# Hashed attention with a mixture of adapters: turning the outputs on TensorE, scaling the signs as a product, and one written-out list of steps

## The chip, the cores and the metric

One Trainium2 chip, of which the kernel uses one core. The metric is the device time of one execution in microseconds (us); for the kernel before it is the median of three runs, and one further execution was profiled.

## The reference

Four batches of eight heads, 768 positions, 64 columns a head. Each row of q and k falls into one of 64 buckets by the signs of six projections; a row attends only to keys of its own bucket. The eight heads of a position are then put side by side as a row x of 512, which goes through the best two of eight adapters of rank 16.

```python
q_bits = (einsum('bhsd,dk->bhsk', q, proj) > 0)      # likewise k_bits; six bits make a bucket
mask = q_bucket[:, :, :, None] == k_bucket[:, :, None, :]
scores = where(mask, scale * q @ k.T, -1e9)
attn_out = softmax(scores) @ v
x = attn_out.transpose(0, 2, 1, 3).reshape(B * S, H * D)
logits = x @ w_gate                                  # 8 experts, the best two, softmax over the two
out = x + sum over the two of  w * ((x @ A[e]) @ B[e])
```

## The kernel before

**Pairs and tiles.** Two heads of a batch make a pair; there are 16 pairs, four to a batch. The scores of all pairs are cut into 144 tiles of 128 x 1024 (`score`, L337), nine to a pair. A tile is made by TensorE in one of three PSUM buffers `s` and turned by ScalarE (ACT) into exponentials in bfloat16 (L343), in the order of the tiles. Tiles 126 to 143 belong to pairs 14 and 15, whose rows are taken in three groups (three, two and one blocks of 128) in turn, so that the last batch can be routed group by group.

**What a tile contracts.** A tile's operands lie in `aug`, with 71 rows: 64 of q or k, and rows 64 to 70 with signs. The signs of the six projections are scaled (`sign`, L201 and L205) so that a pair of rows that differ in a bit gets a large negative score and its exponential vanishes. There are three `aug` buffers beside pair 0's own.

**Preparing a pair.** q and k are loaded in their natural layout (`loadqk`, buffers `nat`), turned in 32 x 32 blocks by VectorE (DVE; `turn32`, L179), cast to bfloat16 by GpSimd (POOL; `rcast`, L232, buffers `rb`) and brought to `aug` by four DMAs (`move`, L241). The projections are float32 products on TensorE (`hash`, L191, in the PSUM pool `n`). The scaled signs reach `aug` through DRAM (`sout`, L211, then `signs`, L218); pairs 0 and 1 bring them straight from SBUF by four DMAs (`sigd`, L221). Pair 0's head 0 has a way of its own (`f0`, `c0`, `g0`, `s0`, `k0`).

**After the exponentials.** Each head's products with v (`pvk`, L358; `pvg`, L378 for the groups) are summed in the PSUM pool `v`, opened by `uni` (L349, L367), a product with 2^-56 that covers rows without a partner. v is cast and summed by POOL (`vcast`, L165 to L170). `norm` (L423, L425) divides into x, in float32, and frees the bank. `to_bf` (L441, POOL) casts a finished pair's 128 columns to `xb`, and `turn` (L432) brings them to `xT` by a crossbar DMA transposition; the groups of the last two pairs are turned by TensorE instead (`turng`, L406) and copied by DVE (L407).

**Routing.** For three blocks of a batch at a time: `lgz` (L451) gives the logits and x A; `route1`, `route_exp` and `route2` find the best two and scale (L462 to L496); `zt` turns the scaled part on TensorE (L509) and copies it (L512); `delta` multiplies by B (L521) and adds x (L525); `store` writes 512 KB or 256 KB.

**What sets the order.** There is no scheduler: each engine takes its instructions in the order in which Python emits them, and waits for what an instruction needs. `plan` attaches steps to tiles (step s of pair p stands behind tile 9p + s), a pair's preparation runs in the two pairs before it (`prep`), and `HEAD`, `LAST` and `END` are lists for the start and the end. Nearly all DMAs go out from SyncE's queue (SP), where a waiting DMA holds all behind it. The pools `n` and `v` have one bank-sized buffer each, `s` three.

Of the kernel before, what the change touches and what calls it, by code (L numbers as in the profile page):

```python
# [22 lines left out]
class Emitter:  # L23


    def __init__(self, ctx, tc, q, k, v, proj, w_gate, A, Bm, out):
# [169 lines left out]
    def sign(self, p, r=slice(0, 128)):  # L196
# [8 lines left out]
        nc.vector.tensor_scalar(out=s2[r], in0=sg[r], scalar1=self.ssc[r], scalar2=None, op0=ALU.mult)  # L205
# [140 lines left out]
    def uni(self, p, h):  # L346
        T, D = self.T, self.D
        pv = self.pv[p, h] = self.ps_v.tile([self.P, T, D + 1], F32, tag="v", name=f"pv{p}_{h}")
        self.nc.tensor.matmul(out=pv, lhsT=self.eps,  # L349
                              rhs=self.vb[p % 3][:, h, T:T + 1, :].to_broadcast([self.P, T, D + 1]),  # L350
                              start=True, stop=False, skip_group_check=True)
# [47 lines left out]
    def turng(self, p, g, where=None):  # L399
        nc, P = self.nc, self.P  # L400
        b, hp = p // self.PPB, p % self.PPB
        i0, n = self.G[g]
        pool, tag = self.bank(where or "n")
        ps = pool.tile([P, n, P], BF16, tag=tag, name=f"xt{p}_{g}")
        for e in range(n):
            nc.tensor.transpose(out=ps[:, e, :], in_=self.xb[p, g][:, e, :], identity=self.ident_bf)  # L406
        nc.vector.tensor_copy(out=self.xT[b][:, hp, i0:i0 + n], in_=ps)  # L407
# [20 lines left out]
    def turn(self, p):  # L428
        if p < 0:
            return  # L430
        b, hp = p // self.PPB, p % self.PPB
        self.nc.sync.dma_start_transpose(out=self.xT[b][:, hp, :, :],  # L432
                                         in_=self.xb[p].rearrange("p t f -> p (t f)"))
# [45 lines left out]
    def route2(self, b, I):  # L479
        if b < 0:  # L480
            return
        nc, P, E, r, n = self.nc, self.P, self.E, self.r, len(I)
# [4 lines left out]
        zm = self.zm[b, I] = self.smallp.tile([P, n, self.ER], BF16, tag=f"zm{n}", name=f"zm{b}_{I[0]}")  # L487
        for i in range(n):
            nc.vector.tensor_tensor(  # L489
                out=zm[:, i, :].rearrange("p (e r) -> p e r", e=E),  # L490
                in0=lz[:, i, E:].rearrange("p (e r) -> p e r", e=E),
                in1=gw[:, i, :].unsqueeze(2).to_broadcast([P, E, r]), op=ALU.mult)
# [4 lines left out]

    def zt(self, b, Is, pool=None):
        if b < 0:
            return  # L500
# [1 line left out]
        n = sum(len(I) for I in Is)
        pool, tag = self.bank(pool or "n")
        ps = pool.tile([P, n, P], BF16, tag=tag, name=f"ztp{b}_{Is[0][0]}")
        zT = self.smallp.tile([P, n, P], BF16, tag=f"zT{n}", name=f"zT{b}_{Is[0][0]}")
        o = 0
        for I in Is:
            for j, i in enumerate(I):
                nc.tensor.transpose(out=ps[:, o, :], in_=self.zm[b, I][:, j, :], identity=self.ident_bf)  # L509
                self.zT[b, i] = (zT[:, o, :], self.rt[b, I][:, j:j + 1])  # L510
                o += 1
        nc.vector.tensor_copy(out=zT, in_=ps)  # L512

    def delta(self, b, i, pool=None):
        if b < 0:
            return
        nc, P = self.nc, self.P
        zT, rt = self.zT[b, i]
        pool, tag = self.bank(pool or "n")
        ps = pool.tile([P, self.Dm], F32, tag=tag, name=f"dl{b}_{i}")  # L520
        nc.tensor.matmul(out=ps, lhsT=zT, rhs=self.Bcat, start=True, stop=True)  # L521
# [3 lines left out]
        nc.vector.scalar_tensor_tensor(out=self.acc[b, u][:, e, :], in0=ps, scalar=rt,  # L525
                                       in1=self.x[b][:, i, :], op0=ALU.mult, op1=ALU.add)
# [201 lines left out]
```

## Time and profile before

| | |
|---|---|
| median of three runs | 192.81 us (190.43 to 193.36) |
| the profiled execution's own time | 191.84 us |
| its span, first to last instruction | 190.0 us |
| mean granted TensorE clock | 0.920 |
| TensorE products busy | 160.2 us, 2059 instructions |
| ScalarE busy | 142.6 us, 164 instructions |
| GpSimd busy | 112.5 us |
| VectorE busy | 110.4 us, 310 instructions |
| first and last exponential start | 8.86 us and 173.9 us |
| moved by DMA | 35.98 MB |

Times in the rows are counted from the span's start. A row of the timeline gives start, length, engine, line of the kernel, operation, output and inputs with their shape and the count; in brackets stands how long the engine was idle before it and who ended that. `PEld` is the loading of weights, `SPq` the issuing of DMAs. A busy TensorE is not TensorE at its peak: products are pipelined, and a row's length has the tail of the last one in it.

### The profile page before, as it was taken

What the parts mean: (1) busy time and instruction counts of PE and PEld (TensorE: products, weight loads), DVE (VectorE), ACT (ScalarE), POOL (GpSimd) and SP (SyncE); (2) the same over time, 40 slices, a digit from 0 to 9 for tenths busy, and PEclk for the clock granted to TensorE, in tenths of its full rate; (3) what the DMA queues carried; (4) which work ended last, traced back from release to release, by engine and by line L of the source; (5) the groups of instructions that cost most, each with busy time, mean ns of one, the idle gap of its engine ahead of it and who ended that gap; (6) DMA issues with size and microseconds to landing.
All of it is one profiled execution on the core that took longest, in us unless ns stands there. A gap on an engine that the chain in (4) does not pass through costs nothing.

```text
span 190.0 us, 5180 instructions
## 1 busy us (share of the span) xinstructions
PE 160.2 (84%) x2059; PEld 106.2 (56%) x2059; DVE 110.4 (58%) x310; ACT 142.6 (75%) x164; POOL 112.5 (59%) x152
## 2 busy tenths in 40 slices
PE   7784989599999979898898997998898998799350
PEld 2432555436576728585666583775666677587210
DVE  4666075411666543757877657087768363868671
ACT  3544759665999996999989989379898997796000
POOL 2879935787789158779590765868754955311000
PEclk9999699855999999999999999589999999999955
DMA  5962369597996969696879999897489782441205
GB/s 144 286 237 49 85 206 292 127 245 119 193 187 142 274 117 298 118 282 153 263 179 265 246 300 170 227 215 250 114 284 292 239 174 85 153 190 39 112 0 221
DMA packets 52836, 35.98 MB, mean 189 GB/s; under 512 B 37060, under 2 KB 49740, under 8 KB 52812
## 3 DMA queue, kind: packets, MB, share of 16 engines
q1 hardware_dynamic: 47756, 35.18, 68.8%
q0 software_dynamic: 4832, 0.27, 4.3%
q8 instruction: 16, 0.26, 0.6%
q10 hardware_dynamic: 224, 0.20, 0.4%
q14 instruction: 8, 0.07, 0.1%
HBM read 20.02 MB, written 6.98 MB: 142 GB/s over the span
## 4 chain that ended last, share of the span: by engine, by line
PE 44%; DVE 19%; DMA 16%; SPq 6%; POOL 5%; issue 4%; ACT 2%; DVEq 0%; POOLq 0%
PE s L337 18%; PE pv L358 9%; DMA aug<-rb 8%; PE hs L191 6%; DMA dr<-s 5%; DVE acc L525 3%; SPq L241 3%; DMA vn<-in_v_dram 3%; DVE R L179 3%; POOL rb L232 2%; PE lz L451 2%; DVE zm L489 2%; PE pv L349 2%; DVE s L205 2%; ACT P L343 2%
## 5 line engine op out<-in xcount | busy, mean ns | idle before, releaser
L343 ACT ACTIVATE P<-s 128x1024 bf16<-128x1024 f32 (+1 forms) x147 | 138.3, 1030 | 28.3 <-PE s L337 27.4
L337 PE MATMUL s<-aug 71*128 71x256 bf16 (+3 forms) x396 | 85.0, 328 | 4.3 <-DMA aug<-rb 3.8
L358 PEld LDWEIGHTS <-P 128*128 128x128 bf16 x1008 | 44.9, 102 | 16.1 <-issue 6.3
L232 POOL CAST rb<-R 128x768 bf16<-128x768 f32 (+1 forms) x32 | 47.5, 1491 | 7.1 <-DVE R L179 6.9
L337 PEld LDWEIGHTS <-aug 71*128 71x128 bf16 x396 | 39.3, 130 | 20.9 <-issue 14.1
L358 PE MATMUL pv<-vb,P 128*128 128x65 bf16 x1008 | 47.3, 199 | 0.0
L165 POOL CAST vb<-vn 128x768 bf16<-128x768 f32 x16 | 13.3, 832 | 36.5 <-DMA vn<-in_v_dram 27.9
L179 DVE STREAM_TRANSPOSE R<-nat 128x384 f32<-128x384 f32 x62 | 31.2, 548 | 2.4 <-DMA nat<-in_k_dram 1.9
L423 DVE RECIPROCAL ri<-pv 128x6 f32<-128x6 f32 x28 | 5.2, 187 | 33.4 <-PE pv L358 33.4
L191 PE MATMUL hs<-R,hst 128*32 128x192 f32 x248 | 20.1, 356 | 4.3 <-DVE zT L512 2.6
L525 DVE SCALAR_TENSOR_TENSOR acc<-dl,rt,x 128x512 f32<-128x512 f32 x24 | 17.5, 744 | 7.1 <-PE dl L521 6.9
L201 DVE TENSOR_SCALAR sg<-hs 128x192 bf16<-128x192 f32 (+1 forms) x16 | 5.7, 358 | 19.0 <-PE hs L191 19.0
L425 DVE TENSOR_TENSOR x<-pv,ri 128x384 f32<-128x384 f32 x28 | 15.6, 557 | 1.0
L167 POOL TENSOR_TENSOR vs<-vn 128x384 f32<-128x384 f32 x16 | 16.0, 1003 | 0.0
L191 PEld LDWEIGHTS hs<-R,hst 128*32 128x32 f32 x248 | 5.9, 111 | 16.0 <-issue 7.4
L349 PE MATMUL pv<-vb,eps 128*128 128x390 bf16 x28 | 9.9, 355 | 4.9 <-DVE x L425 2.7
L441 POOL CAST xb<-x 128x768 bf16<-128x768 f32 x14 | 11.5, 825 | 2.0 <-DVE x L425 1.9
L451 PE MATMUL lz<-wa,xT 128*128 128x136 bf16 x96 | 10.1, 235 | 3.0 <-DVE xT L407 2.5
L205 DVE TENSOR_SCALAR s<-sg,ssc 128x192 bf16<-128x192 bf16 (+1 forms) x16 | 12.3, 768 | 0.6
L521 PE MATMUL dl<-Bcat,zT 128*128 128x512 bf16 x24 | 9.4, 410 | 1.0 <-DVE zT L512 0.5
L397 POOL CAST xg<-x 128x384 bf16<-128x384 f32 (+2 forms) x5 | 2.1, 422 | 12.5 <-DVE x L391 12.5
L451 PEld LDWEIGHTS <-xT 128*128 128x128 bf16 x96 | 6.7, 103 | 3.6 <-issue 2.3
(61 smaller groups left out, 106.3 us busy)
## 6 DMA issues: line engine op xcount, KB each, us to landing
vn<-in_v_dram SPq DMA_DIRECT2D x16, 384.0 KB
nat<-in_q_dram SPq DMA_DIRECT2D x15, 384.0 KB
nat<-in_k_dram SPq DMA_DIRECT2D x15, 384.0 KB
aug<-rb SPq DMA_DIRECT2D x60, 96.0 KB
out_dram<-acc SPq DMA_DIRECT2D x11, 512.0 KB
dr<-s SPq DMA_DIRECT2D x14, 48.0 KB
aug<-dr SPq DMA_DIRECT2D x14, 42.0 KB
out_dram<-acc SPq DMA_DIRECT2D x2, 256.0 KB
```

Of the source, the lines that this page charges most:

```text
L167: nc.gpsimd.tensor_add(out=s3, in0=vn[:, :, 0:3, :], in1=vn[:, :, 3:6, :])
L179: self.nc.vector.transpose(out=self.R[p][:, i, :, h].rearrange("p f t c -> p t f c"), in_=self.nat[p][:, i, h, :].rearrange("p (t f c) -> ...
L191: nc.tensor.matmul(out=self.hs[p][32 * j:32 * j + 32], lhsT=self.hst[:, hf].rearrange("p b i -> p (b i)"), rhs=self.R[p][:, i, hf, h].rear ...
L205: nc.vector.tensor_scalar(out=s2[r], in0=sg[r], scalar1=self.ssc[r], scalar2=None, op0=ALU.mult)
L232: (eng or self.nc.gpsimd).tensor_copy(out=self.rb[p][:, :, :, i].rearrange("p f h (c t) -> p f h c t", t=self.T), in_=self.R[p][:, i, :, h ...
L337: nc.tensor.matmul(out=ps[:, c:c + w * P], lhsT=lhsT, rhs=rhs, start=True, stop=True)
L343: nc.scalar.activation(out=self.P_[p][:, o:o + b - a], in_=ps[:, a:b], func=ACT.Exp, scale=scale)
L349: self.nc.tensor.matmul(out=pv, lhsT=self.eps, rhs=self.vb[p % 3][:, h, T:T + 1, :].to_broadcast([self.P, T, D + 1]), start=True, stop=Fal ...
L358: self.nc.tensor.matmul(out=self.pv[p, h][:, i, :], lhsT=self.P_[p][:, o:o + P], rhs=self.vb[p % 3][:, h, kt, :], start=False, stop=(kt == ...
L425: nc.vector.tensor_tensor(out=self.x[b][:, :, c:c + D], in0=pv[:, :, 0:D], in1=ri.unsqueeze(2).to_broadcast([P, T, D]), op=ALU.mult)
L451: nc.tensor.matmul(out=self.lz[b, I][:, I.index(i), :], lhsT=self.xT[b][:, t, i, :], rhs=self.wa[:, t, :], start=(t == 0 and i == I[0]), s ...
L525: nc.vector.scalar_tensor_tensor(out=self.acc[b, u][:, e, :], in0=ps, scalar=rt, in1=self.x[b][:, i, :], op0=ALU.mult, op1=ALU.add)
```

## The change

Three edits.

1. `turn` is gone. `xtp` turns a pair's six 128 x 128 blocks on TensorE into a PSUM buffer of pool `n` or `s`, and `xtc` copies them to `xT` with DVE. This holds for pairs 0 to 13; the groups of pairs 14 and 15 were turned so before, and their step is now split in the same way (`xtpg`, `xtcg`).
2. In `sign` the scaling is a product of two tensors, the signs and a broadcast column, in place of a tensor by a scalar from memory.
3. `plan`, `prep`, `HEAD`, `LAST` and `END` are replaced by one list, `STEPS`, in which every step of the kernel but the first loads and constants stands in its place. Some steps are cut finer: `route2` into `gate`, `zmul` (one block each) and `gsum`; `zt` into `ztt` and `ztc`; `delta` into `dmm` and `dadd`; `pvk` by one key block. `hash`, `uni`, `unig`, `xtp`, `ztt` and `dmm` take their PSUM pool by name.

```diff
-        nc.vector.tensor_scalar(out=s2[r], in0=sg[r], scalar1=self.ssc[r], scalar2=None, op0=ALU.mult)
+        n = r.stop - r.start
+        nc.vector.tensor_tensor(out=s2[r], in0=sg[r], in1=self.ssc[r].to_broadcast([n, 192]), op=ALU.mult)
...
-    def turn(self, p):
-        self.nc.sync.dma_start_transpose(out=self.xT[b][:, hp, :, :],
-                                         in_=self.xb[p].rearrange("p t f -> p (t f)"))
+    def xtp(self, p, where):
+        pool, tag = self.bank(where)
+        ps = self.xt[p] = pool.tile([P, T, P], BF16, tag=tag, name=f"xt{p}")
+        for t in range(T):
+            nc.tensor.transpose(out=ps[:, t, :], in_=self.xb[p][:, t, :], identity=self.ident_bf)
+
+    def xtc(self, p):
+        b, hp = p // self.PPB, p % self.PPB
+        self.nc.vector.tensor_copy(out=self.xT[b][:, hp], in_=self.xt[p])
...
     def run(self):
         self.start()
-        plan = self.plan()
-        for n in range(9 * self.N):
-            self.score(n)
-            for f, *a in plan.get(n, ()):
-                getattr(self, f)(*a)
-        self.end()
+        for f, *a in STEPS:
+            getattr(self, f)(*a)
...
+STEPS = [
...
+    ("score",81), ("norm",8,0), ("dmm",0,5,"n"),
+    ("score",82),
+    ("score",83), ("turn32",11,1,0), ("dadd",0,5), ("turn32",11,1,1), ("uni",8,1), ("pvk",8,1,(0,)),
...
+]
```

The start on SP's queue. `s21` and `s22` are the scaled signs of pairs 1 and 2, `dr1` and `dr2` their place in DRAM, `rb` the cast rows, `nat` and `vn` the loads of q, k and v. Before:

```order
L221 DMA augf_117<-s20_244 7x4x192 x2
L241 DMA augf_117<-rb0_239 64x2x192 x4
L221 DMA aug1_119<-s21_282 7x4x192 x4
L241 DMA aug1_119<-rb1_268 64x4x192 x4
L146 DMA nat3_321<-in_q_dram 128x2x384
L146 DMA nat3_321<-in_k_dram 128x2x384
L211 DMA dr2_403<-s22_401 128x192
L146 DMA nat4_422<-in_q_dram 128x2x384
L146 DMA nat4_422<-in_k_dram 128x2x384
L241 DMA aug2_120<-rb2_319 64x4x192 x2
L157 DMA vn2_446<-in_v_dram 128x2x384
L218 DMA aug2_120<-dr2_403 7x4x768
```

and in the changed kernel:

```order
L214 DMA dr1_339<-s21_284 128x192
L147 DMA nat3_341<-in_q_dram 128x2x384
L147 DMA nat3_341<-in_k_dram 128x2x384
L221 DMA aug1_119<-dr1_339 7x4x768
L244 DMA aug1_119<-rb1_354 64x4x192 x4
L147 DMA nat4_382<-in_q_dram 128x2x384
L214 DMA dr2_394<-s22_352 128x192
L147 DMA nat4_382<-in_k_dram 128x2x384
L158 DMA vn2_426<-in_v_dram 128x2x384
L244 DMA aug2_120<-rb2_378 64x4x192 x4
L221 DMA aug2_120<-dr2_394 7x4x768
```

Pair 1's signs go through DRAM with the loads of pair 3 between the two steps, and pair 2's four moves stand together, ahead of its signs. (Ahead of these rows the loads of v 0 and v 1 have changed places with those of q and k, and a move of pair 0 stands ahead of `nat2`'s k.)

SP's queue around pairs 10 and 11 in the changed kernel; `acc0_1` is a piece of batch 0's output:

```order
L147 DMA nat12_1975<-in_k_dram 128x2x384
L147 DMA nat13_2042<-in_q_dram 128x2x384
L244 DMA aug2_120<-rb11_1970 64x4x192
L221 DMA aug1_119<-dr10_2000 7x4x768
L244 DMA aug1_119<-rb10_1795 64x4x192
L147 DMA nat14_2150<-in_q_dram 128x2x384
L147 DMA nat13_2042<-in_k_dram 128x2x384
L553 DMA out_0_dram<-acc0_1_1771 128x2x512
```

Before, each pair's loads, its signs, a transposition and its four moves followed one another in a fixed pattern, and no move of a later pair stood ahead of an earlier one's; here a move of pair 11 stands ahead of the signs and the last move of pair 10.

The end on DVE, where the last batch is routed. `dl3_2` is the product of its block 2, `xt15_1` the turned second group of pair 15, `top3_3` begins the routing of blocks 3 and 4. Before:

```order
L525 SCALAR_TENSOR_TENSOR acc3_1_3301<-dl3_2_3299,rt3_0_3217,x3_2615 128x512
L407 COPY xT3_2616<-xt15_1_3303 128x256
L462 MAX top3_3_3316<-lz3_3_3307 128x8 x2
L464 TENSOR_TENSOR d3_3_3319<-lz3_3_3307,top3_3_3316 128x16
L467 TENSOR_TENSOR m3_3_3321<-lz3_3_3307,top3_3_3316 128x16
```

and in the changed kernel:

```order
L415 COPY xT3_2688<-xt15_1_3380 128x256
L394 RECIPROCAL ri14_g2_3396<-pv14_g2_3373 128x2
L396 TENSOR_TENSOR x3_2687<-pv14_g2_3373,ri14_g2_3396 128x128
L475 MAX top3_3_3410<-lz3_3_3401 128x8 x2
L477 TENSOR_TENSOR d3_3_3413<-lz3_3_3401,top3_3_3410 128x16
L480 TENSOR_TENSOR m3_3_3415<-lz3_3_3401,top3_3_3410 128x16
L415 COPY xT3_2688<-xt14_2_3429 128x128
L394 RECIPROCAL ri15_g2_3438<-pv15_g2_3419 128x2
L396 TENSOR_TENSOR x3_2687<-pv15_g2_3419,ri15_g2_3438 128x128
L542 SCALAR_TENSOR_TENSOR acc3_1_3445<-dl3_2_3394,rt3_0_3346,x3_2687 128x512
```

The add of block 2 stood ahead of the copy and of the routing; now it follows both.

More of the change, by code (lines that the diff above doesn't have):

```diff
@@ L397, in normg, with xtpg, xtcg @@
             (nc.gpsimd if eng == "pool" else nc.vector).tensor_copy(out=xb, in_=xv)
-    def turng(self, p, g, where=None):
+    def xtpg(self, p, g, where):
         nc, P = self.nc, self.P
+        n = self.G[g][1]
+        pool, tag = self.bank(where)
+        ps = self.xt[p, g] = pool.tile([P, n, P], BF16, tag=tag, name=f"xt{p}_{g}")
+        for e in range(n):
+            nc.tensor.transpose(out=ps[:, e, :], in_=self.xb[p, g][:, e, :], identity=self.ident_bf)
+    def xtcg(self, p, g):
         b, hp = p // self.PPB, p % self.PPB
         i0, n = self.G[g]
[L403 to L407, printed above, removed]
+        self.nc.vector.tensor_copy(out=self.xT[b][:, hp, i0:i0 + n], in_=self.xt[p, g])
     def newx(self, b):
@@ L486, in route2 @@
         nc.vector.tensor_mul(out=gw, in0=m, in1=e)
[L487 to L492, printed above, removed]
+        self.rg[b, I] = gw
+        self.zm[b, I] = self.smallp.tile([P, n, self.ER], BF16, tag=f"zm{n}", name=f"zm{b}_{I[0]}")
@@ L495, in route2 @@
-        rt = self.rt[b, I] = self.smallp.tile([P, n], F32, tag=f"rt{n}", name=f"rt{b}_{I[0]}")
+        nc.vector.tensor_reduce(out=ss, in_=self.rg[b, I], axis=AX.X, op=ALU.add)
+        rt = self.smallp.tile([P, n], F32, tag=f"rt{n}", name=f"rt{b}_{I[0]}")
         nc.vector.reciprocal(out=rt, in_=ss)
-    def zt(self, b, Is, pool=None):
-        if b < 0:
-            return
-        nc, P = self.nc, self.P
[L502 to L521, printed above, removed]
+        for j, i in enumerate(I):
+            self.rt[b, i] = rt[:, j:j + 1]
+    def ztt(self, b, I, where):
+        nc, P, n = self.nc, self.P, len(I)
+        pool, tag = self.bank(where)
+        ps = self.ztp[b, I] = pool.tile([P, n, P], BF16, tag=tag, name=f"ztp{b}_{I[0]}")
+        for j in range(n):
+            nc.tensor.transpose(out=ps[:, j, :], in_=self.zm[b, I][:, j, :], identity=self.ident_bf)
@@ new lines, in ztc, with dmm @@
+    def ztc(self, b, I):
+        n = len(I)
+        zT = self.smallp.tile([self.P, n, self.P], BF16, tag=f"zT{n}", name=f"zT{b}_{I[0]}")
+        self.nc.vector.tensor_copy(out=zT, in_=self.ztp[b, I])
+        for j, i in enumerate(I):
+            self.zT[b, i] = zT[:, j, :]
+    def dmm(self, b, i, where, n=1):
+        nc, P = self.nc, self.P
+        pool, tag = self.bank(where)
+        ps = pool.tile([P, n, self.Dm], F32, tag=tag, name=f"dl{b}_{i}")
+        for j in range(n):
+            nc.tensor.matmul(out=ps[:, j], lhsT=self.zT[b, i + j], rhs=self.Bcat, start=True, stop=True)
+            self.dl[b, i + j] = ps[:, j]
```

390 lines of the change are left out of this document (265 added, 125 removed), and 9 rows, old and new, of tables (HEAD, STEPS).

## The prediction

> **What bounds the kernel now.** I read the page first: busy shares, the 40 slices with the granted clock.
>
> ```profile
> span 190.0 us, 5180 instructions
> PE 160.2 (84%) x2059; PEld 106.2 (56%) x2059; DVE 110.4 (58%) x310; ACT 142.6 (75%) x164; POOL 112.5 (59%) x152
> PEclk9999699855999999999999999589999999999955
> ```
>
> No engine fills the span. ACT has 142.6 us of work, nearly all of it the exponentials of 144 score tiles; PE comes next; and the clock falls to half in slices 5, 9, 10 and 26 (5 means half speed). So I read next ACT's timeline, where each row after a gap says what ACT waited for.
>
> ```profile
> 25.16 1.02 ACT L343 ACTIVATE P<-s 128x1024 bf16<-128x1024 f32 x1 [2.39 <-PE s L337]
> 35.95 2.08 ACT L343 ACTIVATE P<-s 128x1024 bf16<-128x1024 f32 x2 [1.70 <-PE s L337]
> 38.53 1.02 ACT L343 ACTIVATE P<-s 128x1024 bf16<-128x1024 f32 x1 [0.49 <-PE s L337]
> 40.04 1.02 ACT L343 ACTIVATE P<-s 128x1024 bf16<-128x1024 f32 x1 [0.49 <-PE s L337]
> 46.97 24.30 ACT L343 ACTIVATE P<-s 128x1024 bf16<-128x1024 f32 x26 [0.49 <-PE s L337]
> 72.84 3.10 ACT L343 ACTIVATE P<-s 128x1024 bf16<-128x1024 f32 x3 [1.58 <-PE s L337]
> 121.45 1.02 ACT L343 ACTIVATE P<-s 128x1024 bf16<-128x1024 f32 x1 [2.34 <-PE s L337]
> 126.42 3.76 ACT L343 ACTIVATE P<-s 128x1024 bf16<-128x1024 f32 x4
> 136.95 4.72 ACT L343 ACTIVATE P<-s 128x1024 bf16<-128x1024 f32 x5 [0.52 <-PE s L337]
> 146.14 4.72 ACT L343 ACTIVATE P<-s 128x1024 bf16<-128x1024 f32 x5 [0.52 <-PE s L337]
> 154.16 2.84 ACT L343 ACTIVATE P<-s 128x1024 bf16<-128x1024 f32 x3
> ```
>
> Counting the tiles row by row, 25.16 starts tile 9 (the first of pair 1), 35.95 tile 18 (pair 2), 46.97 tile 25, 72.84 tile 51, 126.42 tile 99, 154.16 tile 126 (the last two pairs). The 26 tiles from 46.97 took 24.30 us: **0.935 us a tile is ACT's own pace**. Against it the span divides into a head (to 25.16), tiles 9 to 51 (47.68 us for 42 tiles, 39.3 at ACT's pace), tiles 51 to 126 (81.32 us for 75, or 1.084 each), and the end (35.84 us from 154.16 to 190.0).
>
> Two stalls with a clock drop behind them stand out. From tile 18 seven tiles took 46.97 - 34.25 = 12.7 us instead of 6.5 (34.25 is 35.95 less the idle 1.70): **6.2 us lost**. From 119.11 (121.45 less 2.34) three tiles took 7.3 us instead of 2.8: **4.5 us lost**. What they waited for:
>
> ```profile
> 30.33 2.47 SPq L241 DMA_DIRECT2D aug<-rb  x2
> 35.24 0.61 PE L337 MATMUL s<-aug 71*128 71x512 bf16 x3 [2.25 <-DMA aug<-rb]
> 109.81 6.13 DMA vn<-in_v_dram
> 118.97 0.48 PE L349 MATMUL pv<-vb,eps 128*128 128x390 bf16 x1 [0.91 <-POOL vb L170]
> 116.00:117.00 1.00, 1.00 (x14) 0.30 (x18) 0.56 (x1) 0.94 (x2) 0.94 (x2) 1.00 1.97 47
> ```
>
> Pair 2's last two pieces of aug were issued at 30.33 and PE stood 2.25 us. In the second stall v's load took 6.13 us to land, POOL cast it late and PE's first product with it waited. The window's last columns are DMA share and GB/s: the queues were full at 47 GB/s while a crossbar transposition was among them.
>
> **What PE needs.** Starts of neighbouring rows give the cost without the pipeline's tail.
>
> ```profile
> 111.16 0.52 PE L451 MATMUL lz<-wa,xT 128*128 128x136 bf16 x6
> 111.52 1.03 PE L337 MATMUL s<-aug 71*128 71x256 bf16 x6
> 127.84 0.33 PE L509 MATMUL ztp<-ident_bf,zm 128*128 128x128 bf16 x3
> 128.01 0.60 PE L337 MATMUL s<-aug 71*128 71x512 bf16 x3
> 129.75 0.64 PE L337 MATMUL s<-aug 71*128 71x512 bf16 x2
> 131.25 0.33 PE L349 MATMUL pv<-vb,eps 128*128 128x390 bf16 x1
> 131.43 0.53 PE L358 MATMUL pv<-vb,P 128*128 128x65 bf16 x12
> 131.79 0.38 PE L521 MATMUL dl<-Bcat,zT 128*128 128x512 bf16 x1
> 132.01 0.60 PE L337 MATMUL s<-aug 71*128 71x512 bf16 x3
> 132.45 0.53 PE L358 MATMUL pv<-vb,P 128*128 128x65 bf16 x12
> ```
>
> A score tile 0.44, twelve pv 0.36, uni 0.18, dl 0.22, lz 0.36/6 = 0.06, one PE transposition 0.17/3 = 0.057. From 129.75 to 131.25 stand two tiles and one half of hash: 1.50 - 0.88 = 0.62. A pair in the middle has 9 x 0.44 + 6 x 0.36 + 2 x 0.18 + 2 x 0.62 and a quarter of its batch's routing, 6 x 0.06 + 1.5 x 0.057 + 1.5 x 0.22: 3.96 + 2.16 + 0.36 + 1.24 + 0.36 + 0.09 + 0.33 = **8.50 us**. ACT needs 9 x 0.935 = 8.42. The undisturbed pair took 146.14 - 136.95 = 9.19. So in the middle PE and ACT are both nearly full, and 0.7 us a pair goes to waits in PE's order.
>
> **The change, part by part.**
>
> ```profile
> L432 SPq DMA_TRANSPOSE xT<-xb x14: 1244/1264/2307, 33.5 to 162.5; - x14
> L205 DVE TENSOR_SCALAR s<-sg,ssc x16: 270/812/1771, 11.1 to 149.7; 128x192 bf16<-128x192 bf16 x15, 64x192 bf16<-64x192 bf16 x1
> L407 DVE COPY xT<-xt 128x384 bf16<-128x384 bf16 x2 | 0.7, 357 | 0.6 <-PE xt L406 0.6
> L489 DVE TENSOR_TENSOR zm<-lz,gw 128x128 bf16<-128x128 f32 x24 | 5.6, 284 | 0.3
> ```
>
> The turn. Removed: 14 crossbar transpositions, 14 x 1.264 = 17.7 us of SP's queue and their DMA time; neither sets the end by itself, so I take nothing for them but shorter landings in the stages below. Added: 84 PE transpositions, 84 x 0.057 = 4.8 us, 0.34 a pair, on an engine that is full in the middle; and 14 copies of 768 columns. No row has such a copy; it lies above the 357 ns of 384 columns and below twice that, 714. I take the middle, 0.54, as part of a copy's time is fixed: 14 x 0.54 = 7.5 us of DVE. The sign scaling. The product of 192 columns isn't in the trace: at least L205's minimum, 270, at most 1.5 times L489's 128 columns, 426; I take 0.35, between the two. By L205's median that saves 16 x (0.81 - 0.35) = 7.4 us. DVE's work stays as it was, and DVE is idle for 42% of the span; without that cover the copies delay the next user of the one-bank PSUM pool, 0.54 a pair.
>
> The order, **head**. Pair 1's signs now go through DRAM (sout, signs) and not straight (four sigd), and its moves stand behind them on SP.
>
> ```profile
> 16.38 3.28 SPq L221 DMA_DIRECT2D aug<-s  x4
> 19.76 2.70 SPq L241 DMA_DIRECT2D aug<-rb  x4
> 150.27 3.31 DMA dr<-s
> ```
>
> Before: signs from 16.38, the last move issued by 22.46, tile 9 on ACT 2.7 us later. After: the first exponential comes later, since POOL casts head 1's rows ahead of head 0's; but head 1's pieces of aug are issued earlier, so tile 4 comes earlier too, and with it hash 1. I put sout at 15 (an estimate, 1.4 ahead of the old signs), its landing at 3.3 us, as in the row, or half of that in an emptier queue; then signs and four moves, five issues of 2.70/4 = 0.675: issued by 20.1 to 21.7, against 19.76 + 2.70 = 22.46. Gain 0.8 to 2.4; I take 1.4. It could also be a loss of 2, were nat 3's loads, now ahead of signs, to land late. Queued behind signs' wait: loads and moves of pairs 1 and 2.
>
> **Tiles 9 to 51.** Pair 2's moves now stand directly behind nat 4 and vn 2 and ahead of its signs, and its casts on POOL follow pair 1's at once. After pair 1's moves, ending at about 21, come five issues and then these four, so they go out at 24 to 26 at the latest; they are needed nine tiles after tile 9, at 23.8 + 8.4 = 32: the first stall goes, 6.2 us, and what is late next is pair 1 itself. I keep 1.5 us over ACT's pace for a half-clock window after that wait: 39.3 + 1.5 = 40.8, a **gain of 6.9** (bounds 8.4 at ACT's pace, 2.2 if as much as the stall is met elsewhere).
>
> **Tiles 51 to 126.** PE's need becomes 8.50 + 0.34 = 8.84, 0.982 a tile. Finer steps put two tiles between a norm and the uni that takes its bank, and v is loaded a pair or more ahead, so the 4.5 us stall should go. I take 1.00 a tile, 75.0 us, a **gain of 6.3**. Bounds: PE's need alone, 73.7 (gain 7.7); the old pace plus the transpositions, (9.19 + 0.34)/9 = 1.059, 79.4 (gain 1.9).
>
> **End.**
>
> ```profile
> 176.67 0.74 DVE L525 SCALAR_TENSOR_TENSOR acc<-dl,rt,x 128x512 f32<-128x512 f32 x1
> 177.33 0.28 DVE L407 COPY xT<-xt 128x256 bf16<-128x256 bf16 x1
> ```
>
> The third add stood just ahead of the copy that the last routing waits for; it now follows that routing: 0.74, with a little for finer steps, 1.0 (bounds -2 to 2.5).
>
> **Sum:** 1.4 + 6.9 + 6.3 + 1.0 = 15.6; span 190.0 - 15.6 = 174.4; the profiled execution's own time was 1.84 above its span, so 176.2. That execution, 191.84, lay 0.5% under the median of the runs, 192.81: **177 us**.
>
> **Rivals.** *PE stays at its old waits.* For: 0.7 us a pair isn't one wait but several; each xtp needs an xb from POOL. Then 1.059 a tile: 177 + 4.4 = 181.5 us.
>
> *One or two stalls remain*, at pair 1 or pair 10. For: signs 10 and the last move of pair 10 stand on SP behind a move of pair 11, which waits for a DVE turn and a POOL cast that follow the add of dl 5, and that product stands ahead of tile 82 on PE.
>
> ```profile
> L179 DVE STREAM_TRANSPOSE R<-nat 128x384 f32<-128x384 f32 x62 | 31.2, 548 | 2.4 <-DMA nat<-in_k_dram 1.9
> L232 POOL CAST rb<-R 128x768 bf16<-128x768 f32 (+1 forms) x32 | 47.5, 1491 | 7.1 <-DVE R L179 6.9
> ```
>
> Product 0.38, add 0.74, turn 0.55, cast 1.49, three issues of 0.675, and 35.24 - 32.80 = 2.4 to land: 7.6 us, and tile 90 is eight tiles or 7.9 us on. Against: that just fits. A stall with its clock drop costs (6.2 + 4.5)/2 = 5.4: 182 with one, 188 with two.
>
> *Slower: the new SP order starves pair after pair.* The same queueing stands at pairs 1, 9 (signs behind a store), 10, 11, 12 and 15. If the landing is 4 us and not 2.4, each of the six stands idle and drops the clock: 177 + 6 x 5.4 = 209. From three stalls on the gain is gone (193), from four it is measurably slower. Against: the 14 transpositions no longer stretch landings.
>
> *The transpositions let the clock fall.* Fourteen times a window of 3.4 us at half clock, where tiles came 1.51 us apart (38.53 to 40.04), not 0.98: 3.4/0.98 - 3.4/1.51 = 1.2 tiles, 14 x 1.2 = 17 us, 194. Against: slices 31 to 37 have 9s with transpositions among their products. [...]
>
> **How the numbers follow.** Forecast 0.55, waits kept 0.17, one or two stalls 0.14, starved 0.07, clock 0.03, better than the forecast's bounds 0.04. A measurement here tells about 2%, so faster means under 189: all but the last two slow cases and part of the stalls, **0.87**; within 2% 0.06, slower 0.07. The low end is the four best bounds together, 2.4 + 8.4 + 7.7 + 2.5 = 21.0, which gives 172, less a margin: 170. The high end holds two stalls: 188.
>
> **What would show it.** Right: tile 9 on ACT at 23 to 24.5; no gap at tile 18; 0.94 a tile to tile 51, then about 1.0; no wait of uni for vn's cast; PE xt about 0.34 us a pair by starts. Wrong: a gap over 2 us on ACT with the half clock behind it after tile 20; middle tiles above 1.05; tile 126 later than 146 us, where the forecast has 139.6 and the trace before 154.16.

## The result and the profile after

The changed kernel takes **176.7 us** (median of six executions, 173.85 to 178.82), the kernel before, in the same stretch on the same chip, 191.56: a ratio of 0.919, 95% interval 0.911 to 0.927. Some executions of either kernel run longer at a lower granted clock (the kernel before 200.15 us at 0.871, against 189.84 at 0.929), and each ratio compares the quicker executions alone. The four executions measured first gave 177.15 and a ratio of 0.919 (0.900 to 0.938). The forecast was 177.0.

The first profiled execution was the longest of its four (183.65 us, with one further wait of TensorE for `aug`, 1.4 us before tile 45, and one of 1.0 us for POOL's cast of `xb` before tile 80); the rows here are of a second one, 176.95 us, near the median. Its page, the lines that stood first for before:

```profile
span 175.2 us, 5325 instructions
PE 154.6 (88%) x2139; PEld 110.5 (63%) x2143; DVE 121.4 (69%) x324; ACT 140.4 (80%) x164; POOL 113.5 (65%) x152
PEclk9999975599999999999999999999999999999995
```

One stretch of half clock is left between the start and the end, in slices 6 to 8 (6 is mixed), where there were two (slices 9 and 10, and 26) and a short one in 5. ACT's timeline, the rows that set the stages:

```profile
25.82 3.06 ACT L346 ACTIVATE P<-s 128x1024 bf16<-128x1024 f32 x3 [3.85 <-PE s L340]
29.92 1.94 ACT L346 ACTIVATE P<-s 128x1024 bf16<-128x1024 f32 x2 [1.03 <-PE s L340]
34.50 19.46 ACT L346 ACTIVATE P<-s 128x1024 bf16<-128x1024 f32 x21 [2.64 <-PE s L340]
...
66.56 6.52 ACT L346 ACTIVATE P<-s 128x1024 bf16<-128x1024 f32 x7 [0.20 <-PE s L340]
...
133.13 11.14 ACT L346 ACTIVATE P<-s 128x1024 bf16<-128x1024 f32 x12 [0.53 <-PE s L340]
...
144.44 3.75 ACT L346 ACTIVATE P<-s 128x1024 bf16<-128x1024 f32 x4
```

Counted as before, 25.82 starts tile 9, 29.92 tile 12, 34.50 tile 14, 66.56 tile 47, 133.13 tile 114, 144.44 tile 126. Tile 18 stands inside a row of 21 without a gap, and from 66.56 to 144.44 no row has more idle time ahead of it than the 0.53 us at 133.13. The gaps are now at tiles 9, 12 and 14: pair 1 is late, and behind it the clock is half. What TensorE waited for there:

```profile
ACT P L346 <- PE s L340: 18.0, 22, 3.9
PE s L340 <- DMA aug<-rb: 4.6, 1, 4.6
```

It waited once in the whole run for moved rows of `aug`, 4.6 us, where tile 9 begins. The stages against the forecast (tile 51 is the fifth of the seven from 66.56, at 70.2):

| stage | before, us | after, us | gain | forecast |
|---|---|---|---|---|
| start to tile 9 | 25.16 | 25.82 | -0.7 | 1.4 |
| tiles 9 to 51 | 47.68 | 44.4 | 3.3 | 6.9 |
| tiles 51 to 126 | 81.32 | 74.2 | 7.1 | 6.3 |
| tile 126 to the end | 35.84 | 30.8 | 5.1 | 1.0 |
| span | 190.0 | 175.2 | 14.8 | 15.6 |

**The sum was right; three of its four terms were not.** The head and the end lie outside the bounds that they were given, and tiles 9 to 51 brought half of the gain forecast. 5.7 us were missing up to tile 51 and 4.9 too many came behind it; that the two nearly cancel is luck. The costs of the added work, from the groups (busy us and mean ns of one) and from TensorE's timeline:

```profile
L446 DVE COPY xT<-xt 128x768 bf16<-128x768 bf16 x14 | 7.6, 544 | 2.5 <-PE xt L442 2.5
L208 DVE TENSOR_TENSOR s<-sg,ssc 128x192 bf16<-128x192 bf16 (+1 forms) x16 | 14.6, 911 | 0.6
```

```profile
143.97 0.50 PE L442 MATMUL xt<-ident_bf,xb 128*128 128x128 bf16 x6
144.32 0.60 PE L340 MATMUL s<-aug 71*128 71x128 bf16 x4
```

Six transpositions take 0.35 us by starts (0.34 forecast), the copy 544 ns (0.54 forecast). The product of signs takes 911 ns, not 350. VectorE's busy time rose from 110.4 to 121.4 us, where the forecast had it stay; 7.6 us of that are the copies.

### The profile page after: what moved, and what is told of

It is laid out like the page before. It is cut to its first block, busy times and chain, and to the rows that moved or that the text cites. A ratio compares the mean times of both kernels' runs of the same rounds, so it can differ in the third digit from the quotient of the medians.

```text
span 181.9 us, 5325 instructions
## 1 busy us (share of the span) xinstructions
PE 161.8 (89%) x2139; PEld 114.5 (63%) x2143; DVE 120.3 (66%) x324; ACT 140.8 (77%) x164; POOL 113.8 (63%) x152
## 4 chain that ended last, share of the span: by engine, by line
PE 54%; DMA 15%; DVE 13%; ACT 6%; SPq 5%; issue 2%; POOL 2%; DVEq 0%; POOLq 0%
PE s L340 24%; PE pv L362 11%; DMA aug<-rb 8%; PE hs L193 7%; ACT P L346 6%; SPq L244 4%; PE lz L464 3%; DVE s L208 2%; PE pv L353 2%; DMA nat<-in_q_dram 2%; DMA dr<-s 2%; DMA vn<-in_v_dram 2%; DVE acc L542 2%; PE xt L442 2%; PE pv_g L383 2%
## 5 line engine op out<-in xcount | busy, mean ns | idle before, releaser
L346 ACT ACTIVATE P<-s 128x1024 bf16<-128x1024 f32 (+1 forms) x147 | 136.4, 1024 | 24.8 <-PE s L340 24.4
L340 PE MATMUL s<-aug 71*128 71x256 bf16 (+3 forms) x396 | 80.3, 329 | 6.9 <-DMA aug<-rb 5.9
L340 PEld LDWEIGHTS <-aug 71*128 71x128 bf16 x396 | 41.6, 129 | 23.1 <-issue 9.8
L362 PEld LDWEIGHTS <-P 128*128 128x128 bf16 x1008 | 42.4, 103 | 7.7 <-issue 2.4
L362 PE MATMUL pv<-vb,P 128*128 128x65 bf16 x1008 | 44.6, 201 | 0.1
L180 DVE STREAM_TRANSPOSE R<-nat 128x384 f32<-128x384 f32 x62 | 32.5, 554 | 6.3 <-DMA nat<-in_q_dram 3.6
L193 PE MATMUL hs<-R,hst 128*32 128x192 f32 x248 | 17.3, 371 | 0.0
L433 DVE TENSOR_TENSOR x<-pv,ri 128x384 f32<-128x384 f32 x28 | 15.6, 557 | 1.0
L208 DVE TENSOR_TENSOR s<-sg,ssc 128x192 bf16<-128x192 bf16 (+1 forms) x16 | 14.1, 882 | 0.6
L446 DVE COPY xT<-xt 128x768 bf16<-128x768 bf16 x14 | 7.6, 543 | 2.7 <-PE xt L442 2.7
L464 PE MATMUL lz<-wa,xT 128*128 128x136 bf16 x96 | 8.5, 222 | 0.2
```

The costliest lines, as they stand in the source:

```text
L180: self.nc.vector.transpose(out=self.R[p][:, i, :, h].rearrange("p f t c -> p t f c"), in_=self.nat[p][:, i, h, :].rearrange("p (t f c) -> ...
L193: nc.tensor.matmul(out=self.hs[p][32 * j:32 * j + 32], lhsT=self.hst[:, hf].rearrange("p b i -> p (b i)"), rhs=self.R[p][:, i, hf, h].rear ...
L208: nc.vector.tensor_tensor(out=s2[r], in0=sg[r], in1=self.ssc[r].to_broadcast([n, 192]), op=ALU.mult)
L340: nc.tensor.matmul(out=ps[:, c:c + w * P], lhsT=lhsT, rhs=rhs, start=True, stop=True)
L346: nc.scalar.activation(out=self.P_[p][:, o:o + b - a], in_=ps[:, a:b], func=ACT.Exp, scale=scale)
L362: self.nc.tensor.matmul(out=self.pv[p, h][:, i, :], lhsT=self.P_[p][:, o:o + P], rhs=self.vb[p % 3][:, h, kt, :], start=False, stop=(kt == ...
```

## The experiments

Twelve runs, in four groups; medians are of six executions, and the kernel before was measured in each group. Its median was 191.56 beside the changed kernel again, the scalar scaling, the crossbar and the turn in the old order; 193.27 beside the later crossbar, the later turn, the products of zeros and the old end; 191.50 beside the later loads, the three edits and the signs in PSUM; 192.94 beside the last run at pair 1.

### The changed kernel again

> The changed kernel once more, nothing edited. Theory A (waits in the new order of SP's queue): PE's wait for pair 1's last pieces of aug, about 4 us before tile 9, stands again at the same place with a window of half clock behind it, because it follows from the order; those at tiles 45 and 81 are there too, or smaller. 174 to 178 us. Rival B (the waits of the first profile belong to one disturbed execution): tile 9 starts before 24.5 us, and no wait of PE for aug is over 1 us; the time is then 171 to 175.

176.69 us; its profile is the one shown above. The wait of 4.6 us for pair 1 stands again, with half clock from 24.5 to 34.7, so it belongs to the order, as theory A had it. The other two waits of the first execution (the second stood before tile 80, not 81 as the expectation has it) do not come back, and ACT stands 1.0 us before tile 41 instead: these vary from execution to execution.

### The scaling of the signs as before

```diff
-        nc.vector.tensor_tensor(out=s2[r], in0=sg[r], in1=self.ssc[r].to_broadcast([n, 192]), op=ALU.mult)
+        nc.vector.tensor_scalar(out=s2[r], in0=sg[r], scalar1=self.ssc[r], scalar2=None, op0=ALU.mult)
```

> The changed kernel with the scaling of the signs as before, a tensor by a scalar from memory; order and turning as changed. Theory A (the product of tensors is no cheaper: 0.88 us a piece against 0.77 in the profiles so far, and it is off the path): within 1 us of the changed kernel in time, the scaling 0.7 to 0.9 us a piece. Rival, the step of the prediction: the product costs 0.35 and saves 7.4 us of VectorE; going back costs 0 to 2 us in time and raises VectorE's busy time by 7.

176.22 us (174.38 to 177.80), ratio to before 0.922 (0.916 to 0.928): the product is worth nothing. VectorE's busy time falls by 2.9 us (121.4 to 118.5), where the step of the prediction has it rise by 7. The two forms by line, minimum, median and maximum in ns, the scalar form first and the changed kernel's second:

```profile
L207 DVE TENSOR_SCALAR s<-sg,ssc x16: 270/559/3000, 10.8 to 138.2; 128x192 bf16<-128x192 bf16 x15, 64x192 bf16<-64x192 bf16 x1
```

```profile
L208 DVE TENSOR_TENSOR s<-sg,ssc x16: 355/709/3167, 10.7 to 140.7; 128x192 bf16<-128x192 bf16 x15, 64x192 bf16<-64x192 bf16 x1
```

At its quickest the product is the slower one. The long ones have a pattern, seen in the timeline of the scalar run:

```profile
18.51 3.00 DVE L207 TENSOR_SCALAR s<-sg,ssc 128x192 bf16<-128x192 bf16 x1
...
19.66 0.83 POOL L166 CAST vb<-vn 128x768 bf16<-128x768 f32 x1
...
20.45 0.99 POOL L168 TENSOR_TENSOR vs<-vn 128x384 f32<-128x384 f32 x1
```

The scaling ends at 21.51, POOL's instruction at 21.44, and three POOL instructions ran behind one another meanwhile. In before too, twelve of the sixteen take longer than 270 ns, and each of these ends 0.06 to 0.08 us behind a POOL instruction (30.26 + 1.04 = 31.30, POOL's cast at 31.24).

### The signs kept in PSUM

```diff
-            self.hs[p] = pool.tile([self.P, 192], F32, tag=tag, name=f"hs{p}")
+            self.hs[p] = pool.tile([self.P, 384], F32, tag=tag, name=f"hs{p}")
...
-        sg = self.sgp.tile([P, 192], BF16, tag="sg", name=f"sg{p}")
+        sg = self.hs[p][:, 192:384]
...
-        nc.vector.tensor_tensor(out=s2[r], in0=sg[r], in1=self.ssc[r].to_broadcast([n, 192]), op=ALU.mult)
+        nc.vector.tensor_scalar(out=s2[r], in0=sg[r], scalar1=self.ssc[r], scalar2=None, op0=ALU.mult)
```

> The changed kernel with the unscaled signs kept in PSUM in float32 and the scaling a tensor by a scalar from there, so that it has no tensor input in SBUF. Theory I (the scaling, in either form, cannot run while a POOL instruction runs: 0.27 and 0.36 us without one, and otherwise it ends about 0.07 us behind POOL's): it becomes 0.3 to 0.4 us with no long ones, none above 0.5, and VectorE's busy time falls by 6 to 9 us; time 0 to 1 us shorter, since VectorE is not the bound. Rival (the long ones come from something else on VectorE): its maximum stays above 1 us.

```profile
L207 DVE TENSOR_SCALAR s<-hs,ssc x16: 416/418/423, 12.4 to 143.2; 128x192 bf16<-128x192 f32 x15, 64x192 bf16<-64x192 f32 x1
```

All sixteen take 416 to 423 ns, beside POOL or not, and VectorE's busy time falls from 121.4 to 113.6 us: theory I holds, with a somewhat higher base than expected. The time does not fall: 177.07 us (175.52 to 179.45). What the prediction hoped to save was really saved here, 7.8 us of VectorE, and it was worth nothing.

### The crossbar in the new order

The turning alone is undone, at the copy's place in the list and, in a second run, five tiles later:

```diff
     def xtp(self, p, where):
+        pass
...
     def xtc(self, p):
-        self.nc.vector.tensor_copy(out=self.xT[b][:, hp], in_=self.xt[p])
+        self.nc.sync.dma_start_transpose(out=self.xT[b][:, hp, :, :],
+                                         in_=self.xb[p].rearrange("p t f -> p (t f)"))
```

> The changed kernel with pairs 0 to 13 turned by the crossbar transposition on SP's queue at the place of the copy xtc, and no products xtp; list and product of signs as changed. Theory A (the list brings the gain, the turning on TensorE brings nothing by itself): PE has 4.8 us less, SP 17.7 us more; 176 to 183 us. Rival C (the crossbar in SP's queue and its DMA traffic were what held the kernel back, by long landings and late moves): 188 us or more, with PE's waits for aug back at many pairs.

197.81 us (194.77 to 201.83), ratio 1.027 (1.020 to 1.034): theory A falls. The new order with the crossbar is slower than the kernel before. SP's waits in the line of the transposition (each is for POOL's cast of `xb`; the name is that of POOL's instruction that ended last; with two smaller ones 37.3 us in all) and TensorE's for `aug`:

```profile
SPq L441 <- POOL vb L166: 15.9, 3, 7.0
SPq L441 <- POOL xb L450: 10.3, 6, 4.3
SPq L441 <- POOL vs L168: 9.7, 3, 7.2
```

```profile
PE s L340 <- DMA aug<-rb: 12.8, 4, 5.4
```

and SP ahead of tile 81, the first of pair 9:

```profile
100.84 0.55 SPq L549 DMA_DIRECT2D out_dram<-acc  x1
105.81 1.24 SPq L441 DMA_TRANSPOSE xT<-xb  x1
107.11 0.48 SPq L221 DMA_DIRECT2D aug<-dr  x1
```

SP stood 4.4 us for the transposition, and pair 9's signs were queued behind it. This is the rival "the new SP order starves pair after pair", with a store and a transposition where the prediction had a move. Is it the waiting, or the transposition itself? The second run takes most of the waiting away:

> As the run with the crossbar in the new list (197.8 us), but each transposition is issued five tiles later in the list, when POOL has long made its xb. Theory E (the loss there was SP's queue standing for xb: 15.9 + 10.3 + 9.7 us of SP's waits in the line of the transposition, with moves and signs queued behind): the waits in that line fall below 5 us, the stalls at pairs 5, 9 and 10 go, 177 to 183 us. Rival C (the transposition's own 1.26 us of queue and its traffic make the moves late wherever it stands): 188 us or more.

```profile
SPq L441 <- POOL xb L450: 3.0, 2, 1.8
SPq L441 <- POOL vb L171: 2.1, 3, 1.0
```

With three smaller ones SP's waits there fall from 37.3 us to 9.2, TensorE's for `aug` only from 12.8 to 10.2, and the time to 186.85 us (185.46 to 191.61; ratio 0.980, 0.963 to 0.998), between the two theories. So of the 21 us between this order with the crossbar (197.8) and without it (176.7), **about 11 went with three quarters of SP's standing for `xb`, and 10 stay** with a transposition that still waits 9.2 us in all. (By the ratios to the kernel before, 1.027, 0.980 and 0.919, it is 9 and 12.) Behind the start the largest stalls are then at tiles 45, 47, 63 and 90. But 2 us are lost by tile 18 already (it starts at 40.1 us, in the changed kernel at 38.1), and the first transposition was issued at 37.6, so not all of the 10 need be the transposition's. Whether the rest comes from 1.24 to 2.07 us of queue for each transposition, from the waits that are left or from its traffic was not separated.

### The turn on TensorE in the old order

The kernel before, with only the turning changed; the six products and the copy stand at the crossbar's step, and in a second run seven tiles behind the cast, by `put(p + 1, 1, ("turn", p - 1))`.

```diff
-        self.nc.sync.dma_start_transpose(out=self.xT[b][:, hp, :, :],
-                                         in_=self.xb[p].rearrange("p t f -> p (t f)"))
+        ps = self.ps_n.tile([P, T, P], BF16, tag="n", name=f"xt{p}")
+        for t in range(T):
+            nc.tensor.transpose(out=ps[:, t, :], in_=self.xb[p][:, t, :], identity=self.ident_bf)
+        nc.vector.tensor_copy(out=self.xT[b][:, hp], in_=ps)
...
-            put(p, 5, ("turn", p - 1))
+            put(p, 5 if p < N - 2 else 7, ("turn", p - 1))
```

> The kernel before with one edit: each pair 0 to 13 is turned by six products on TensorE and a copy by VectorE at the step where the crossbar stood (two steps later for pair 13, since the bank is taken). Theory A: the stall at tile 18 stays (6.2 us), that at tile 96 may go (4.5 us), PE gets 4.8 us more work and one more wait a pair: 186 to 194 us. Rival C: without the crossbar in SP's queue landings shorten and the time falls to 182 or less.

196.15 us (194.10 to 201.51), ratio 1.026 (1.018 to 1.034): slower than before, 2 us above theory A's range and far from rival C's. TensorE and ACT at tile 60, with a like gap of ACT at each ninth tile from 51 to 123 (1.05 to 1.27 us, and 3.55 at tile 51):

```profile
80.74 0.64 PE L337 MATMUL s<-aug 71*128 71x256 bf16 x3
81.28 0.49 PE L435 MATMUL xt<-ident_bf,xb 128*128 128x128 bf16 x6
82.84 0.40 PE L454 MATMUL lz<-wa,xT 128*128 128x136 bf16 x4 [0.52 <-DVE xT L436]
83.07 0.60 PE L337 MATMUL s<-aug 71*128 71x512 bf16 x3
83.71 1.02 ACT L343 ACTIVATE P<-s 128x1024 bf16<-128x1024 f32 x1 [1.27 <-PE s L337]
```

Between two score tiles stand here the transpositions, a uni, twelve pv and, once the copy has freed the bank, routing: 2.3 us from tile to tile, where ACT needs 0.94.

> As the run with the old order and the turn on TensorE (196.2 us), but the six products stand seven tiles behind the cast to_bf in place of two. Theory F (the loss there is one wait a pair of TensorE, 1.1 us at tiles 51, 60, 69 and so on to 123, for POOL's cast and then for the bank that the copy frees): the gaps at these tiles go and the time falls by about 8 x 1.1 = 9 to 186 to 189 us. Rival: the gap moves to the new place, because TensorE has no room in a pair; 194 us or more.

194.10 us (193.42 to 201.51), ratio 1.021 (1.010 to 1.031): theory F falls. The gaps at tile 60 and its like go, and others come at tiles 65, 74, 83 and so on, at the new place:

```profile
93.71 0.60 PE L337 MATMUL s<-aug 71*128 71x512 bf16 x2
94.72 0.49 PE L435 MATMUL xt<-ident_bf,xb 128*128 128x128 bf16 x6 [0.41 <-DVE acc L528]
95.42 0.61 PE L337 MATMUL s<-aug 71*128 71x256 bf16 x3
96.06 2.88 ACT L343 ACTIVATE P<-s 128x1024 bf16<-128x1024 f32 x3 [0.70 <-PE s L337]
```

From one score tile to the next it is 1.71 us here (93.71 to 95.42), with the transpositions, twelve pv and a wait of 0.41; neither of the two places tried in the old order has room for them. Tiles 51 to 126 took 85.0 and 84.6 us in these two runs, 74.2 in the changed kernel with the same transpositions.

### The wait at pair 1

Filling it with products of zeros into an idle bank:

```diff
+    def fill(self, n):
+        ps = self.ps_n.tile([self.P, 512], F32, tag="n", name="fill")
+        for i in range(n):
+            self.nc.tensor.matmul(out=ps, lhsT=self.wz[:, 0:128], rhs=self.wz[:, 0:512], start=True, stop=True)
...
-    ("score",9),
+    ("fill",16), ("score",9),
```

> The changed kernel with 16 extra products of zeros (128 x 512, 3.4 us at full clock, result not used) on TensorE between tiles 8 and 9, where it stood 4.2 us waiting for pair 1's last piece of aug. Theory A: the wait for aug stays, but the half clock behind it goes, and tiles 9 to 14 take 4.7 to 5.5 us in place of 8.7: 172 to 174 us in all. Rival D (the clock falls for another reason, or the gaps at tiles 12 and 14 are waits of their own order): the clock still drops at about 24.5 us or tiles 9 to 14 still take over 8 us, and the time stays at 176 or rises by the products.

```profile
PEclk9999999999999999999999999999999999999965
```

```profile
20.09 3.40 PE L254 MATMUL fill<-wz 128*128 128x512 bf16 x15
24.41 1.04 PE L345 MATMUL s<-aug 71*128 71x512 bf16 x5 [0.92 <-DMA aug<-rb]
```

173.64 us (171.75 to 176.09), ratio 0.907 (0.882 to 0.933); 15 of the 16 products have a record in the trace. Pair 1 comes nearly as late as before (tile 9 at 25.05 us, above at 25.82), the clock stays full until the end, and tiles 9 to 14 take 5.2 us in place of 8.7: theory A. The intervals of the ratios overlap; the stage itself shows the 3.5 us.

Then what makes pair 1 late. Two loads move behind its four moves:

```diff
-    ("score",5), ("hash",2,0,(0,1),"s"), ("hash",2,1), ("sout",1), ("loadqk",3,0), ("loadqk",3,1), ("signs",1),
+    ("score",5), ("hash",2,0,(0,1),"s"), ("hash",2,1), ("sout",1), ("signs",1),
...
-    ("score",7), ("move",1,2), ("move",1,3), ("move",1,1), ("turn32",3,0,0), ("move",1,0),
+    ("score",7), ("move",1,2), ("move",1,3), ("move",1,1), ("move",1,0), ("loadqk",3,0), ("loadqk",3,1), ("turn32",3,0,0),
```

> The changed kernel with the two loads of nat 3 (768 KB) issued behind pair 1's four moves and not ahead of its signs. Theory G (these loads are what makes pair 1 late: the DMA engines were 99% busy at 350 GB/s from 18 to 22 us, and pair 1's moves took 5.9 us to land in place of 2.4): moves land in about 3 us, TensorE's wait before tile 9 falls from 4.2 to about 2 us and tile 9 starts 1.5 to 3 us earlier, 22.5 to 23.5; 173.5 to 175.5 us in all if the half clock stays, less if it goes. Rival H (the issue of the five DMAs on SP, about 0.9 us each with its gap, sets it): tile 9 moves by less than 0.7 us, and the time stays at 176.5 or rises as pair 3 is later.

178.51 us (175.17 to 180.67), not better. SP, TensorE, VectorE and ACT from one timeline:

```profile
15.51 0.36 SPq L214 DMA_DIRECT2D dr<-s  x1
18.52 0.31 SPq L221 DMA_DIRECT2D aug<-dr  x1
18.92 2.64 SPq L244 DMA_DIRECT2D aug<-rb  x4
```

```profile
23.62 1.47 PE L340 MATMUL s<-aug 71*128 71x512 bf16 x5 [3.74 <-DMA aug<-rb]
25.26 0.58 DVE L180 STREAM_TRANSPOSE R<-nat 128x384 f32<-128x384 f32 x1 [3.45 <-DMA nat<-in_q_dram]
28.07 0.15 DVE L431 RECIPROCAL ri<-pv 128x6 f32<-128x6 f32 x1
28.88 0.51 PE L353 MATMUL pv<-vb,eps 128*128 128x390 bf16 x1 [2.61 <-DVE x L433]
30.94 1.94 ACT L346 ACTIVATE P<-s 128x1024 bf16<-128x1024 f32 x2 [3.60 <-PE s L340]
```

From the issue of the first of the four moves to TensorE's first product with them it is 4.7 us here, and 4.9 in the next two runs, which keep this edit. With the loads ahead it is 6.6 to 7.9 us in seven profiles and 4.7 in one. So the loads held the moves up in most executions, as theory G says, although the DMA engines were full from 18 to 20 us alone and not to 22 (busy shares of 0.98 from 18 to 20 and 0.59 from 20 to 22 in the changed kernel's first profile). But SP now stood 2.6 us for the trip of the signs through DRAM (1.2 in the next two runs), which the loads had covered, and tile 9, at 24.27, gained little: with the loads ahead it starts at 24.1 to 26.4 us in six profiles. And a new wait came: VectorE stood for pair 3's rows, the norm of pair 0 was queued behind those turns, uni on TensorE waited for the norm, and ACT stood 3.6 us before tile 12, where it stood 1.0 in the changed kernel.

> Three edits together on the changed kernel: the loads of nat 3 behind pair 1's moves, 8 extra products of zeros on TensorE ahead of tile 9 (1.7 us at full clock), and the signs kept in PSUM. If theories A, G and I hold: tile 9 at 22.5 to 23.5 us, no half clock before the end, 170 to 172.5 us. If H holds instead: 172.5 to 174.5 by the products alone; if 8 products don't hold the clock, 173.5 to 175.5.

The edit adds 8 products of zeros ahead of tile 9 and the signs in PSUM. 176.52 us (174.42 to 180.53): outside all three guesses. Tile 9 came at 22.60, as G has it, and the same late tile 12 (4.01 us idle) then cost the gain. Last, that wait alone is taken away:

```diff
-    ("score",8), ("rcast",2,0), ("turn32",3,1,0), ("turn32",3,1,1), ("loadqk",4,0), ("turn32",3,0,1), ("rcast",2,1),
-        ("vcast",1), ("rcast",3,0), ("sout",2), ("load_moe",0),
+    ("score",8), ("rcast",2,0), ("loadqk",4,0), ("rcast",2,1), ("vcast",1), ("sout",2), ("load_moe",0),
...
-    ("score",10), ("pvk",0,0,(5,)), ("norm",0,0),
+    ("score",10), ("pvk",0,0,(5,)), ("norm",0,0), ("turn32",3,0,0), ("turn32",3,0,1), ("rcast",3,0), ("turn32",3,1,0),
+        ("turn32",3,1,1),
```

> The three edits of the run before, and pair 3's four turns on VectorE (with the cast of its q) moved behind the norm of pair 0's first head. Theory J (in the two runs with the later loads tile 12 came 3 to 4 us late because that norm stood on VectorE behind turns that waited for nat 3, and uni of pair 0's second head on TensorE waited for the norm): the gap before tile 12 falls to about 1 us, no half clock stands behind it, tiles 9 to 14 take 5 to 6 us in place of 10.8, 170 to 172.5 us in all. Rival (pair 3 is now simply late, wherever its turns stand): the gap moves to tile 14 with the hash of pair 3, and the time stays at 174 to 177.

```profile
22.44 4.69 ACT L350 ACTIVATE P<-s 128x1024 bf16<-128x1024 f32 x5 [1.26 <-PE s L344]
27.95 4.05 ACT L350 ACTIVATE P<-s 128x1024 bf16<-128x1024 f32 x4 [0.82 <-PE s L344]
```

173.19 us (171.13 to 176.78), ratio 0.907 (0.897 to 0.918); tiles 9 to 14 take 5.5 us in place of 10.8, and the gap before tile 12 is gone. Theory J holds in the trace; the median is 0.7 us over its range. This version and the one with the products alone are the quickest measured, about 3 us under the changed kernel, and cannot be told apart.

### The end in the old order

Behind tile 143 the steps are put back into the order of the kernel before:

```diff
-        ("pvg",14,2,7,8), ("pvg",14,2,8,9), ("xtcg",15,1), ("pvg",14,2,9,10), ("pvg",14,2,10,11), ("pvg",14,2,11,12),
-        ("dmm",3,2,"s"), ("normg",14,2), ("lgz",3,(3,4),3,(0,1,2,3),"s"), ("lgz",3,(3,4),4,(0,1,2,3)),
-        ("route1",3,(3,4)), ("route_exp",3,(3,4)), ("unig",15,2), ("pvg",15,2,0,1), ("pvg",15,2,1,2),
...
+        ("dmm",3,2,"s"), ("dadd",3,2), ("xtpg",15,1,"n"), ("xtcg",15,1), ("lgz",3,(3,4),3,(0,1,2,3)),
+        ("lgz",3,(3,4),4,(0,1,2,3)), ("route1",3,(3,4)), ("route_exp",3,(3,4)), ("xtpg",14,2,"s"), ("xtcg",14,2),
+        ("lgz",3,(5,),5,(0,1,2),"s"), ("unig",15,2), ("pvg",15,2,0,12), ("normg",15,2,"act"), ("gate",3,(3,4)),
...
```

> The changed kernel with the steps behind tile 143 in the order of the kernel before. Theory A (the end's gain is the new order of DVE and PE there: from the last exponential to the last add 11.05 us before, 7.75 after): 2.5 to 4 us longer, 179 to 180.5. Rival, the step of the prediction: only the third add's place counts, 0.7 to 1.0 us longer, 177.3 to 177.8.

180.39 us (176.83 to 180.84). The execution with the profile is the quickest, the only one under 179.8; the stage is read from it. Its last exponential starts at 159.91 of a span of 175.06, so 15.15 us from there to the end; in the changed kernel 163.05 of 175.2, 12.1; before 173.88 of 190.0, 16.1. The copy of pair 15's group 1 shows where the first of it went, in this run and then in the changed kernel:

```profile
161.86 0.74 DVE L542 SCALAR_TENSOR_TENSOR acc<-dl,rt,x 128x512 f32<-128x512 f32 x1
162.51 0.28 DVE L415 COPY xT<-xt 128x256 bf16<-128x256 bf16 x1
```

```profile
164.59 0.28 DVE L415 COPY xT<-xt 128x256 bf16<-128x256 bf16 x1
```

The copy stands behind the third add and starts 2.6 us behind the start of the last exponential; in the changed kernel it starts 1.5 us behind. The 1.1 us grow to 3.0 over the routing that follows. Theory A holds: 3.0 of the 5.1 us are this order, not the 0.7 of one add.

## Why the prediction was right, and where it was not

**What bounds the kernel** held: with the stalls gone, ACT and TensorE are both nearly full from tile 54 to 126 (busy for 95 and 97% of it).

**The turn.** The prices held (0.35 for 0.34, 0.544 for 0.54). The step that failed is "neither sets the end by itself, so I take nothing for them but shorter landings in the stages below", about the 17.7 us of crossbar on SP. In the new order the crossbar costs 10 to 21 us; in the old order its replacement costs 4 to 5 net (ratios 1.021 and 1.026), since TensorE had no room at the places tried. Medians, us (the two runs marked later stand beside 193.3 for the kernel before, the others beside 191.6):

| | crossbar on SP | turned on TensorE |
|---|---|---|
| old order | 191.6 | 196.2; later in the pair 194.1 |
| new order | 197.8; later in the list 186.9 | 176.7 |

**Where they stand, neither edit gains alone; together they gain 15 us.** Only with the crossbar moved five tiles later does the order gain by itself, 2% (ratio 0.980, 0.963 to 0.998). The prediction added the parts up term by term and has no term for this dependence; the sum came out because the corner with both was the one built.

**The sign scaling.** The forecast 0.35 is what the product takes with POOL idle (355 ns at least). The saving of 7.4 us of VectorE is what failed: L205's median of 0.81 was mostly waiting for POOL, and the product waits as well (in the changed kernel's first profile its long ones end 0.21 to 0.27 us behind a POOL instruction). L205's row, from 270 to 1771 ns, would have said so, had its long ones been held against POOL's timeline. By form it is 355 to 3167 ns with two SBUF inputs, 270 to 3000 in the scalar form from SBUF, 416 to 423 with the tensor input in PSUM. The longest, 18.94 to 22.11 us, ends 0.22 us behind the third POOL instruction that it overlaps.

**Head.** Forecast 1.4, measured -0.7. Over six profiles with this head tile 9 starts at 24.1 to 26.4 us, over three with the old one at 25.2 to 25.4, so on average there was no gain. SP's rows:

```profile
17.33 0.31 SPq L221 DMA_DIRECT2D aug<-dr  x1
17.73 4.50 SPq L244 DMA_DIRECT2D aug<-rb  x4
```

The landing of the signs in DRAM held, and was quicker than either value taken: `sout` was issued at 15.78, `signs` at 17.33. The term failed behind it, at the four moves. Their issue took 4.50 us, not 2.70 (2.64 to 4.50 over the profiles with this head), and tile 9 came on ACT 3.6 us behind it, not 2.7. What held them, as far as these runs show it, was mostly the 768 KB of nat 3, the loss that the prediction named beside its value and did not take: with those loads later, tile 9 started at 22.60 and 22.44 in two runs (which also have the signs in PSUM and the products of zeros), and at 24.27 in the third.

**Tiles 9 to 51.** The first stall went, as forecast, and pair 1 became the late one, as forecast; its price was mis-sized: 1.5 us taken over ACT's pace, 5.1 measured. 3.5 of these went when the wait was filled, and the filled run took 39.4 us for the stage, ACT's pace. The half clock behind the wait lasted 10.2 us (in the first profile from 23.1 to 33.3), where the shortest stretch in the trace before lasted 3.4 (19.5 to 22.9). That trace had shown it: behind the stall at tile 18 the clock was half from 36.6 to 46.8 us, 10.2 as well.

**Tiles 51 to 126.** 0.99 us a tile, forecast 1.00, between the floor of 0.982 and the bound of 1.059. No uni waited there for v. The run with the scalar scaling took 73.7 us, PE's need itself.

**End.** 1.0 taken, 5.1 measured, outside the bound of 2.5. The term counted one add; the order of copies and products behind tile 143 gave 3.0, and about 1.1 came between tiles 126 and 143. The remaining 1.0 is not accounted for.

**The rivals.** *PE stays at its old waits* is out in the new order. *One or two stalls* came at pair 1, and in one execution also at pair 5 and before tile 80, not at pair 10. *Starved* did not come in the changed kernel, and did when the crossbar was put back into its queue. *The transpositions let the clock fall* did not come: with the wait at pair 1 filled, the clock stayed full from the start until behind the last exponential, across all fourteen turns, each with 0.35 us of transpositions at a time.
